# Splitting w_out into two float16 parts in place: the low part over the weights, the high part by a DMA, with the first stage in another order

## Chip, cores, metric

One core of a Trainium2 chip. The metric is the device time of one execution in microseconds. The core has TensorE (PE, matmuls, and its weight loads PEld), VectorE (DVE), ScalarE (ACT), GpSimd (POOL) and SyncE (SP), whose queue issues all DMAs of this kernel.

## What is computed

Attention in two steps, then a gated MLP with an RMS norm in front:

```python
q, k, v: (8 batches, 8 heads, 576 tokens, 64);  p: (8, 8, 32, 64)
packed = softmax(p @ k.T / 8) @ v               # 32 packed tokens a head
out    = softmax(q @ packed.T / 8) @ packed
x  = out.transpose(0, 2, 1, 3).reshape(4608, 512)
xn = x / sqrt(mean(x * x) + 1e-6) * rms_g
y  = (silu(xn @ w_gate) * (xn @ w_val)) @ w_out # 512 -> 1536 -> 512
```

The weights arrive as 64-bit floats and are read as pairs of 32-bit words; the result is float32.

## The kernel before

The 4608 tokens are worked through in 12 units of 384. For each unit there are a query load, an attention, and an MLP of 12 column blocks (`ft`) in six pairs (`c`). A batch has 576 tokens, so that some units need the packed tokens of two batches ("mixed" units). To keep float32 accuracy at float16 speed, each operand is split into a high and a low float16 part, and each product is made of three matmuls (high x high, high x low, low x high).

**The MLP.** The packed tokens are multiplied with the gate and value weights first (`packed_weights`, line 1217), and the result is split into `ring` (`pw_evict`, lines 455 and 457). The MLP's first part is the matmuls of line 1607; `gated` takes its results through silu (ACT, line 1658), a multiplication (DVE, line 1661), the high part (ACT, line 1681) and the low part (DVE line 1687 or POOL line 1684) into `hall`. The second part (line 1643) multiplies `hall` with `wo`, the two parts of w_out; `store` brings the result out (lines 1699 and 1702).

**Preparing the weights.** Each weight comes in pieces of 1 MB (twelve for gate and value, `gv_piece`, loads on line 530; six for w_out, `wo_piece`, loads on line 625). The raw words land in memory that is used later for something else (`ring`, `wo32` and `hall`; `RAW_AT` and `WO_AT` say which room). `to_f32` makes float32 of them: an ACT instruction (line 490), a POOL or DVE shift (lines 495 and 500; the lists `LOW` and `LOW_WO` choose) and a DVE merge (lines 497 or 502). Then come sums of squares for the scales. When all scales of w_out are known (`wo_scale`), `wo_split` makes the high and the low part of each of the six pieces: a scaling into a free `big` room (ACT line 690 or DVE line 693), the high part (ACT, line 699) and the low part (POOL, line 705). Both parts of a row lie in the 2,048 bytes that its float32 values had.

**Batches.** For each batch `keysets` loads p (line 734) and the keys in two halves (line 716) and turns them (early batches on PE, line 793, with evictions on line 800). `stage1` makes the packed tokens. The attention of a unit ends in `aTu` (line 1321), from which its MLP starts; lines 1513 to 1535 are its RMS norm on the way.

**The order.** Nothing is scheduled at run time: every engine's queue is written out in advance. Each piece of work is a generator (a chain) that yields what it wants next: an engine and an estimated time, a free buffer (a `Room` by name), or a mark set by another chain. `Plan.run` keeps an estimated clock for each engine and picks, among the chains that could start within a window (`CHOICE`) of the first, the one of the lowest rank (`RANK`, plus `LATER` times its number). The first dictionary of each pair is for the first stage (until unit 1's attention is planned), the second for the rest. `LATENCY`, `ACT_COST`, `DVE_COST`, `TABLE` and the like are its estimates; they change the order of instructions and nothing else. Where PE would idle in the first stage, `fill` puts in matmuls on constants (line 1731). `KEYS_AFTER` names the weight load after which batch 1's loads may be planned:

```python
if b == 1 and KEYS_AFTER:
    yield ("issued", KEYS_AFTER)
```

Loads 0 to 11 are the gate and value pieces, from 12 on those of w_out. There are six `big` rooms (p, keys, values, queries and their turned forms) and two `o` rooms (squares, and the stored results).

Of the kernel before, what the change touches and what calls it, by code (L numbers as in the profile page):

```python
# [9 lines left out]
F32 = mybir.dt.float32  # L10
F16 = mybir.dt.float16
# [3 lines left out]
AF = mybir.ActivationFunctionType  # L15
ALU = mybir.AluOpType
AX = mybir.AxisListType

P = 128
# [5 lines left out]
PE, ACT, DVE, POOL, LOAD, TPOSE = "pe", "act", "dve", "pool", "load", "tpose"  # L25

EXP, SILU = "exp", "silu"
# [3 lines left out]
    mybir.EngineType.SP,  # L31
)

LATENCY = {PE: 0.293, ACT: 0.16, EXP: 0.16, SILU: 0.16, DVE: 0.14, POOL: 0.022}
# [12 lines left out]

LOADING = (2.0, 320e3, 0.8)
TURNING = 2.2
# [3 lines left out]
def pe(n, count):  # L53

    return count * max(n / 2400 + 0.0025, 0.029)

ACT_COST = (0.076, 0.87e-3)
DVE_COST = (0.098, 0.953e-3)  # L60
# [173 lines left out]

RANK = ({"mlp": 1e9, "scales": 0.68, "gated": 0, "pw_evict": 0.42, "store": 0, "attention": 0.32, "stage1": 0.84, "keys": 0.49, "v": 0, "query": 0.55, "pw": 0.44, "g": 1.01, "w": 1.56, "wo": 0.96, "wo_split": 1.49, "conv": 2.38}, {"mlp": 1e9, "scales": 0.03, "gated": 0, "pw_evict": 0, "store": 0.25, "attention": 1.21, "stage1": 0.58, "keys": 0.27, "v": 0.78, "query": 0.42, "pw": 1.72, "g": 2.14, "w": 0.92, "wo": 2.54, "wo_split": 0.63, "conv": 2.76})
# [12 lines left out]
LOW_WO = "PPPDPP"  # L250

NORM_BY = "AAGAAAAAAAAA"
WO_SQ = "AAAAAA"
WO_BY = "ADADDD"
WO_LO = "PPPPPP"
KEYS_AFTER = 9
KEYS_BY = "ADAAAAADAADA"
QUERY_BY = "AADADA"
H_HI = "AAAAAAAAAAAA"
WO_HI = "AAAAAA"  # L260
H_LO = "DDDPPDDDDDDP"

H_LO_MIXED = "DDDDDDDDDDDD"
H_LO_ONE = "DDDDDDDDDDDD"


NORM_SLACK = (1.284, 3.0)

PW16_FROM = 8

# [16 lines left out]
def tile_packed_attention_then_swiglu(  # L287
# [36 lines left out]
    NFT = DF // P  # L324
# [101 lines left out]
    def tiny(n=1):  # L426

        r = plan.rooms["tiny"].pop(0)
        plan.rooms["tiny"].append(r)
        return r[1][:, :n, 0]  # L430

    def trio():
        r = plan.rooms["trio"].pop(0)
# [247 lines left out]
    def wo_split(i):  # L681
        yield "wo_sc",
        if H32:
            yield ("wo_free", i)
        st0 = yield Room("big")
        st = st0[:, : 2 * DM].rearrange("p (f n) -> p f n", f=2)
        hl = wo[:, 2 * i : 2 * i + 2]
        if WO_BY[i] == "A":
            yield ACT, act(1024)
            nc.scalar.activation(st, wo32[:, 2 * i : 2 * i + 2, :], AF.Copy, scale=wo_sc[:, i : i + 1])  # L690
        else:
            yield DVE, dve(1024) * 0.6
            nc.vector.tensor_scalar_mul(st, wo32[:, 2 * i : 2 * i + 2, :], wo_sc[:, i : i + 1])
        if WO_HI[i] == "D":
            yield DVE, 0.62
            nc.vector.tensor_copy(hl[:, :, 0, :], st)
        else:
            yield ACT, act(1024)
            nc.scalar.copy(hl[:, :, 0, :], st)
        if WO_LO[i] == "D":  # L700
            yield DVE, dve(1024)
            nc.vector.tensor_tensor(hl[:, :, 1, :], st, hl[:, :, 0, :], ALU.subtract)
        else:
            yield POOL, pool(1024)
            nc.gpsimd.tensor_tensor(hl[:, :, 1, :], st, hl[:, :, 0, :], ALU.subtract)
        plan.give("big", st0)
        plan.mark("wo_hl", i)


# [867 lines left out]
    def mlp():  # L1577
        for u in range(NU):
            yield ("aTu", u)
            if u == 0:  # L1580
                plan.warm = True
            sc, aT = units[u]
            for ft in range(NFT):
                c, f = divmod(ft, 2)
                for b, _, o, n in parts(u):
                    yield ("pw", b, c)
                yield ("sc", 0, c) if u == 0 else ("sc", u)
                pss, done = [], []
                for w in range(2):
                    ps = yield Room("pm")  # L1590
                    psi = ps[:, :UT].rearrange("p (i t) -> p i t", i=TPU)
                    yield PE, pe(UT, 8 if PW32 and u == 0 else 7 if PW32 and u == 1 else 6)
                    for b, _, o, n in parts(u):
                        pw = ring[:, slot_of(b, c)]
                        if PW32 and b == 0:
                            pw = pw.rearrange("p e l w f -> p e (l w f)").bitcast(F32)
                            x = aths[0] if u else whole(aT)
                            for g in range(2):
                                nc.tensor.matmul(
                                    psi[:, :, o : o + n], pw[:, g, 2 * P * w + f * P : 2 * P * w + (f + 1) * P], x[:, :, g, :],  # L1600
                                    start=(g == 0), stop=(g == 1),
                                )
                            continue
                        j = 0
                        for g in range(2):
                            for lw, la in ((0, 0), (0, 1), (1, 0)):
                                nc.tensor.matmul(  # L1607
                                    psi[:, :, o : o + n], pw[:, g, lw, w, f * P : (f + 1) * P], aT[:, :, la, g, o : o + n],
                                    start=(j == 0), stop=(j == 5),
                                )  # L1610
                                j += 1
                    pss.append(ps)
                    done.append(plan.now)
                plan.add(gated(u, ft, pss, done), "gated", u, ft)
                if f == 1:
                    for b, *_ in parts(u):
                        if (u + 1) * UT >= (b + 1) * S:
                            plan.mark("used", b, c)
            plan.give("aTu", aT)
            plan.mark("po", u)  # L1620
            for i in range(TPU):
                po = yield Room("pm")
                n = 0
                ts = slice(i * P, (i + 1) * P)
                if H32 and u == 0:
                    for ft in range(NFT):
                        if i == 0:
                            yield ("h", u, ft)
                            yield ("wo32", ft // 2)
                        yield PE, pe(DM, 4)  # L1630
                        nc.tensor.matmul(po, hall32[:, ft, ts], wo32[:, ft, :], start=(ft == 0), stop=(ft == NFT - 1))
                        if i == TPU - 1 and ft % 2:
                            plan.mark("wo_free", ft // 2)
                    plan.add(store(u, i, po), "store", u, i)
                    continue
                for ft in range(NFT):
                    if i == 0:
                        yield ("h", u, ft)
                        if u == (1 if H32 else 0):
                            yield ("wo_hl", ft // 2)  # L1640
                    yield PE, pe(DM, 3)
                    for lh, lw in ((0, 0), (0, 1), (1, 0)):
                        nc.tensor.matmul(po, hall[:, ft, lh, ts], wo[:, ft, lw, :], start=(n == 0), stop=(n == 3 * NFT - 1))  # L1643
                        n += 1
                plan.add(store(u, i, po), "store", u, i)

# [137 lines left out]
```

## Time and profile before

| | |
|---|---|
| median of 3 runs | 783.03 us (782.7 to 784.86) |
| the profiled execution | 781.74 us, its span 780.0 us |
| granted TensorE clock, mean | 0.987 |
| PE busy | 742.0 us (95%) |
| DVE busy | 497.2 us (64%) |
| ACT busy | 469.1 us (60%) |
| POOL busy | 55.5 us (7%) |

Times in the lines of the profile are microseconds from the span's start. In a timeline a row gives start, duration, engine, line, operation, what is written and read with the shapes, and in brackets how long the engine had idled and who released it. In the rows of waits stand who waited for whom, the sum, the number of times and the longest.

### The profile page before, as it was taken

Reading aid. Unit: us, or ns where it says so; the run is one execution under the profiler, and the core shown is the slowest. Engines: PE = TensorE matmul, PEld = TensorE weight load, DVE = VectorE, ACT = ScalarE, POOL = GpSimd, SP = SyncE. Lnnn points to the kernel's source line nnn. Section 1 sums busy time; section 2 is a strip of 40 time slices with the busy share of each in tenths; the row PEclk is TensorE's granted clock in tenths of the full one; section 3 lists DMA queues with packets and bytes.
Section 4 is the critical chain, followed back from the end, with each engine's and each line's share of the span. In section 5 each row is a group of like instructions: output and inputs, shape, how many; then the busy total and the mean of one; then the engine's idle time right before and its main releaser. Section 6 shows DMA issues by size and latency. Waiting matters only on the chain.

```text
span 780.0 us, 18192 instructions
## 1 busy us (share of the span) xinstructions
PE 742.0 (95%) x7653; PEld 433.5 (56%) x7653; DVE 497.2 (64%) x1086; ACT 469.1 (60%) x889; POOL 55.5 (7%) x55
## 2 busy tenths in 40 slices
PE   8756898999999999999999999999999999999998
PEld 6633463676445555477455555576554455685553
DVE  1798878586777486469467674688467365472341
ACT  3677877677778567288467756487366255371230
POOL 1433045000000000000000000000000000000000
PEclk9896999999999999999999999999999999999999
DMA  9998412545476437423832670837213213400001
GB/s 257 386 271 240 153 55 75 96 102 127 95 157 95 105 66 154 110 64 57 195 93 51 107 181 3 159 67 152 69 38 59 68 35 73 90 13 24 27 1 41
DMA packets 135506, 82.18 MB, mean 105 GB/s; under 512 B 98432, under 2 KB 123008, under 8 KB 135424
## 3 DMA queue, kind: packets, MB, share of 16 engines
q1 hardware_dynamic: 135424, 81.02, 44.2%
q8 instruction: 60, 0.98, 0.5%
q14 instruction: 22, 0.18, 0.1%
HBM read 47.97 MB, written 9.44 MB: 74 GB/s over the span
## 4 chain that ended last, share of the span: by engine, by line
PE 83%; DVE 6%; DMA 4%; SPq 3%; ACT 2%; issue 1%; DVEq 0%; ACTq 0%
PE pm_1x L1607 10%; PE pm_0x L1643 10%; PE pm_2x L1643 10%; PE pm_2x L1607 9%; PE pm_3x L1607 8%; PE pm_1x L1643 8%; PE pm_0x L1607 8%; PE pm_3x L1643 7%; SPq L530 2%; DMA hall<-in_moe_w_gate_dram 2%; PE pm_3x L1217 2%; PE pm_0x L1217 2%; PE quad L1426 1%; PE quad L1066 1%; PE pm_1x L1217 1%
## 5 line engine op out<-in xcount | busy, mean ns | idle before, releaser
L1607 PEld LDWEIGHTS <-ring 128*128 128x128 f16 x2304 | 204.7, 98 | 105.6 <-issue 33.6
L1643 PEld LDWEIGHTS <-hall 128*128 128x128 f16 x1296 | 124.1, 98 | 151.4 <-issue 11.7
L1643 PE MATMUL pm_0x<-wo,hall 128*128 128x512 f16 x360 | 82.2, 379 | 0.0
L1643 PE MATMUL pm_2x<-wo,hall 128*128 128x512 f16 x360 | 81.2, 379 | 0.0
L1643 PE MATMUL pm_3x<-wo,hall 128*128 128x512 f16 x288 | 65.2, 379 | 0.9 <-DVE t_1x L1661 0.9
L1643 PE MATMUL pm_1x<-wo,hall 128*128 128x512 f16 x288 | 65.1, 379 | 0.0
L1681 ACT CAST hall<-t_1x 128x384 f16<-128x384 f32 x72 | 36.7, 510 | 37.4 <-DVE t_1x L1661 36.9
L1607 PE MATMUL pm_1x<-aTu_0x,ring 128*128 128x192 f16 (+1 forms) x402 | 55.0, 281 | 1.2 <-DVE t_0x L1661 1.2
L1681 ACT CAST hall<-t_0x 128x384 f16<-128x384 f32 x72 | 36.5, 507 | 25.7 <-DVE t_0x L1661 25.4
L1687 DVE TENSOR_TENSOR hall<-t_1x,hall 128x384 f16<-128x384 f32 x70 | 38.9, 555 | 12.3 <-ACT hall L1681 10.4
L1687 DVE TENSOR_TENSOR hall<-t_0x,hall 128x384 f16<-128x384 f32 x71 | 39.7, 559 | 10.4 <-ACT hall L1681 10.2
L1607 PE MATMUL pm_2x<-aTu_0x,ring 128*128 128x384 f16 (+1 forms) x276 | 43.4, 298 | 0.0
L1607 PE MATMUL pm_0x<-aTu_1x,ring 128*128 128x384 f16 (+1 forms) x288 | 42.3, 289 | 1.0 <-DVE tiny_68x L963 1.0
L1607 PE MATMUL pm_2x<-aTu_1x,ring 128*128 128x192 f16 (+1 forms) x300 | 42.4, 285 | 0.6 <-DVE t_0x L1661 0.6
L1607 PE MATMUL pm_1x<-aTu_1x,ring 128*128 128x192 f16 (+1 forms) x300 | 42.3, 284 | 0.0
L1607 PE MATMUL pm_3x<-aTu_1x,ring 128*128 128x192 f16 (+1 forms) x264 | 37.8, 286 | 0.0
L1607 PE MATMUL pm_3x<-aTu_0x,ring 128*128 128x384 f16 (+1 forms) x240 | 35.5, 290 | 1.3 <-DVE t_0x L1661 0.9
L1607 PE MATMUL pm_0x<-aTu_0x,ring 128*128 128x192 f16 (+1 forms) x234 | 31.0, 277 | 1.6 <-ACT t_0x L1658 1.2
L1519 POOL TENSOR_TENSOR trio_2x<-trio_1x,neghalf 128x3 f32<-128x3 f32 x6 | 5.5, 916 | 280.9 <-DVE trio_1x L1513 280.9
L1519 POOL TENSOR_TENSOR trio_6x<-trio_5x,neghalf 128x3 f32<-128x3 f32 x6 | 5.1, 850 | 271.4 <-DVE trio_5x L1513 271.4
L1497 ACT ACTIVATE quad<-quad 128x512 f32<-128x512 f32 x36 | 21.1, 585 | 4.6 <-PE quad L1489 4.1
L457 DVE SCALAR_TENSOR_TENSOR ring<-pm_3x,pw_sc,ring 128x512 f16<-128x512 f32 x28 | 20.8, 744 | 3.8 <-ACT ring L455 3.8
(893 smaller groups left out, 1288.4 us busy)
## 6 DMA issues: line engine op xcount, KB each, us to landing
out_dram<-o_1x SPq DMA_DIRECT2D x18, 256.0 KB, 2.0
out_dram<-o_0x SPq DMA_DIRECT2D x18, 256.0 KB, 2.2
hall<-in_moe_w_out_dram SPq DMA_DIRECT2D x4, 1024.0 KB, 8.7
big_3x<-in_k_dram SPq DMA_DIRECT2D x7, 576.0 KB, 6.7
wo<-in_moe_w_gate_dram SPq DMA_DIRECT2D x3, 1024.0 KB, 15.5
wo<-in_moe_w_val_dram SPq DMA_DIRECT2D x3, 1024.0 KB, 13.0
big_2x<-in_k_dram SPq DMA_DIRECT2D x5, 576.0 KB, 6.3
big_1x<-in_v_dram SPq DMA_DIRECT2D x4, 576.0 KB, 7.3
```

The lines of the kernel that those rows point to most:

```text
L457: nc.vector.scalar_tensor_tensor(lo, x, s, hi, ALU.mult, ALU.subtract)
L530: nc.sync.dma_start(raw.rearrange("p k n e -> p k (n e)"), (w_gate, w_val)[n][:, 4 * c * P : 4 * (c + 1) * P].rearrange("(kt p) f -> p kt ...
L1066: nc.tensor.matmul(pp[32 * j : 32 * j + 32, :D], a1T[:, c, 32 * j : 32 * j + 32], vf[:, j, cv, :], start=(c == 0), stop=(c == NCK - 1),)
L1217: nc.tensor.matmul(ps[e][32 * j : 32 * j + 32, :], pg[h, j, :], wgv[h, c, j, :, :].rearrange("p w f -> p (w f)"), start=True, stop=True,)
L1426: nc.tensor.matmul(ps2[o : o + n, i, :, pi, :], qT[:, lq, i, pi, o : o + n], packs[b][3][:, lp, pi, :, :], start=(j == 0), stop=(j == 2),)
L1497: nc.scalar.activation(x, x, AF.Square, scale=2.0**-14, accum_out=ss[:, i : i + 1])
L1519: nc.gpsimd.tensor_tensor(ru, var, neghalf.broadcast_to([P, TPU]), ALU.pow)
L1607: nc.tensor.matmul(psi[:, :, o : o + n], pw[:, g, lw, w, f * P : (f + 1) * P], aT[:, :, la, g, o : o + n], start=(j == 0), stop=(j == 5),)
L1643: nc.tensor.matmul(po, hall[:, ft, lh, ts], wo[:, ft, lw, :], start=(n == 0), stop=(n == 3 * NFT - 1))
L1681: nc.scalar.copy(hall[:, ft, 0, :], t)
L1687: nc.vector.tensor_tensor(hall[:, ft, 1, :], t, hall[:, ft, 0, :], ALU.subtract)
```

## The change

`wo_split` no longer copies the scaled weights into a `big` room. ACT scales the piece and writes its high part into an `o` room; one DVE instruction multiplies the piece by its scale, subtracts the high part and writes the low part over the first half of each row of the weights; a DMA then brings the high part over the second half. The output matmuls read the two halves in the other order. Beside it, lists of which engine does what, the rooms of w_out's raw pieces, the place of batch 1's loads, the layout of the small scalars (`tiny`) and the planner's numbers are changed.

```diff
-CHOICE = ({'pe': 0.0, 'act': 0.458, 'dve': 0.275, 'pool': 0.476, 'sp': 1.005}, {'pe': 0.0, 'act': 0.417, 'dve': 0.087, 'pool': 0.208, 'sp': 0.274})
+CHOICE = ({'pe': 0.0, 'act': 0.458, 'dve': 0.275, 'pool': 0.298, 'sp': 0.833}, {'pe': 0.0, 'act': 0.382, 'dve': 0.13, 'pool': 0.269, 'sp': 0.274})
-AGE = (0.1, 0.078)
-TABLE = 1.735
+AGE = (0.1, 0)
+TABLE = 1.554
...
-RANK = ({"mlp": 1e9, "scales": 0.68, "gated": 0, "pw_evict": 0.42, "store": 0, "attention": 0.32, "stage1": 0.84, "keys": 0.49, "v": 0, "query": 0.55, "pw": 0.44, "g": 1.01, "w": 1.56, "wo": 0.96, "wo_split": 1.49, "conv": 2.38}, ...
-LATER = {"attention": -0.1, "stage1": -0.4, "keys": -0.05, "query": 0.0, "pw": -0.34, "w": 0.04, "wo": 0.0, "wo_split": 0.04}
+RANK = ({"mlp": 1e9, "scales": 0, "gated": 0, "pw_evict": 0.63, "store": 0, "attention": 0.16, "stage1": 0.84, "keys": 0.18, "v": 0, "query": 0.3, "pw": 0.44, "g": 1.01, "w": 1.45, "wo": 1.05, "wo_split": 1.49, "conv": 2.38}, ...
+LATER = {"attention": -0.78, "stage1": -0.4, "keys": 0.45, "query": 0.4, "pw": -0.46, "w": 0.34, "wo": 0.0, "wo_split": 0.02}
-WO_AT = (7, 8, 3, 8, 3, 8)
+WO_AT = (7, 3, 8, 7, 3, 8)
-VAL_BY = "DDPDDD"
+VAL_BY = "DDPADD"
-LOW_WO = "PPPDPP"
+LOW_WO = "PPPDDP"
-KEYS_AFTER = 9
+KEYS_AFTER = 12
-H_HI = "AAAAAAAAAAAA"
+H_HI = "AAAADAAAAADA"
-H_LO_MIXED = "DDDDDDDDDDDD"
+H_LO_MIXED = "DDDDPDDDDDDD"
...
-    rooms("tiny", 96, [P, 2, 2], F32)
+    rooms("tiny", 96, [P, 2], F32)
...
     def wo_split(i):
         yield "wo_sc",
-        st0 = yield Room("big")
-        st = st0[:, : 2 * DM].rearrange("p (f n) -> p f n", f=2)
-        hl = wo[:, 2 * i : 2 * i + 2]
...
-            nc.gpsimd.tensor_tensor(hl[:, :, 1, :], st, hl[:, :, 0, :], ALU.subtract)
-        plan.give("big", st0)
+        x, sc = wo32[:, 2 * i : 2 * i + 2, :], wo_sc[:, i : i + 1]
+        hi0 = yield Room("o")
+        hi = hi0.bitcast(F16).rearrange("p (f n) -> p f n", f=2)
+        yield ACT, act(1024)
+        nc.scalar.activation(hi, x, AF.Copy, scale=sc)
+        yield DVE, dve(1024)
+        nc.vector.scalar_tensor_tensor(wo[:, 2 * i : 2 * i + 2, 0, :], x, sc, hi, ALU.mult, ALU.subtract)
+        yield LOAD, P * 2048
+        nc.sync.dma_start(wo[:, 2 * i : 2 * i + 2, 1, :], hi)
+        plan.give("o", hi0)
...
-    nc.tensor.matmul(po, hall[:, ft, lh, ts], wo[:, ft, lw, :], ...)
+    nc.tensor.matmul(po, hall[:, ft, lh, ts], wo[:, ft, 1 - lw, :], ...)
```

More of the change, by code (lines that the diff above doesn't have):

```diff
@@ L32 @@
 )
-LATENCY = {PE: 0.293, ACT: 0.16, EXP: 0.16, SILU: 0.16, DVE: 0.14, POOL: 0.022}
+LATENCY = {PE: 0.299, ACT: 0.16, EXP: 0.16, SILU: 0.16, DVE: 0.14, POOL: 0.006}
 SLACK = (0.317, 0.223)
-CHOICE = ({'pe': 0.0, 'act': 0.458, 'dve': 0.275, 'pool': 0.476, 'sp': 1.005}, {'pe': 0.0, 'act': 0.417, 'dve': 0.087, 'pool': 0.208, 'sp': 0.274})
+CHOICE = ({'pe': 0.0, 'act': 0.458, 'dve': 0.275, 'pool': 0.298, 'sp': 0.833}, {'pe': 0.0, 'act': 0.382, 'dve': 0.13, 'pool': 0.269, 'sp': 0.274})
 IN_TURN = range(18)
 FILL = (0.9, 1.0, 400.0, 0.6)
-AGE = (0.1, 0.078)
-TABLE = 1.735
+AGE = (0.1, 0)
+TABLE = 1.554
 LOADING = (2.0, 320e3, 0.8)
@@ L55, in pe @@
     return count * max(n / 2400 + 0.0025, 0.029)
-ACT_COST = (0.076, 0.87e-3)
-DVE_COST = (0.098, 0.953e-3)
+ACT_COST = (0.081, 0.87e-3)
+DVE_COST = (0.068, 0.953e-3)
 def act(n):
@@ L233, in run @@
             self.go(chain)
-RANK = ({"mlp": 1e9, "scales": 0.68, "gated": 0, "pw_evict": 0.42, "store": 0, "attention": 0.32, "stage1": 0.84, "keys": 0.49, "v": 0, "query": 0.55, "pw": 0.44, "g": 1.01, "w": 1.56, "wo": 0.96, "wo_split": 1.49, "conv": 2.38}, {"mlp": 1e9, "scales": 0.03, "gated": 0, "pw_evict": 0, "store": 0.25, "attention": 1.21, "stage1": 0.58, "keys": 0.27, "v": 0.78, "query": 0.42, "pw": 1.72, "g": 2.14, "w": 0.92, "wo": 2.54, "wo_split": 0.63, "conv": 2.76})
-LATER = {"attention": -0.1, "stage1": -0.4, "keys": -0.05, "query": 0.0, "pw": -0.34, "w": 0.04, "wo": 0.0, "wo_split": 0.04}
+RANK = ({"mlp": 1e9, "scales": 0, "gated": 0, "pw_evict": 0.63, "store": 0, "attention": 0.16, "stage1": 0.84, "keys": 0.18, "v": 0, "query": 0.3, "pw": 0.44, "g": 1.01, "w": 1.45, "wo": 1.05, "wo_split": 1.49, "conv": 2.38}, {"mlp": 1e9, "scales": 0.03, "gated": 0, "pw_evict": 0, "store": 0.25, "attention": 1.21, "stage1": 0.58, "keys": 0.27, "v": 0.78, "query": 0.42, "pw": 1.83, "g": 2.14, "w": 0.92, "wo": 2.54, "wo_split": 0.63, "conv": 2.76})
+LATER = {"attention": -0.78, "stage1": -0.4, "keys": 0.45, "query": 0.4, "pw": -0.46, "w": 0.34, "wo": 0.0, "wo_split": 0.02}
 RAW_AT = (0, 1, 2, 3, 4, 5, 6, 7, 8, 4, 5, 6)
-WO_AT = (7, 8, 3, 8, 3, 8)
+WO_AT = (7, 3, 8, 7, 3, 8)
 EARLY_ROOMS = (5, 4, 3)
@@ L429, in tiny @@
         plan.rooms["tiny"].append(r)
-        return r[1][:, :n, 0]
+        return r[1][:, :n]
     def trio():
@@ L684, in wo_split @@
             yield ("wo_free", i)
-        st0 = yield Room("big")
-        st = st0[:, : 2 * DM].rearrange("p (f n) -> p f n", f=2)
-        hl = wo[:, 2 * i : 2 * i + 2]
[L688 to L705, printed above, removed]
-        plan.give("big", st0)
+        x, sc = wo32[:, 2 * i : 2 * i + 2, :], wo_sc[:, i : i + 1]
[8 more added lines that the diff above has]
+        plan.give("o", hi0)
         plan.mark("wo_hl", i)
@@ L1642, in mlp @@
                     for lh, lw in ((0, 0), (0, 1), (1, 0)):
-                        nc.tensor.matmul(po, hall[:, ft, lh, ts], wo[:, ft, lw, :], start=(n == 0), stop=(n == 3 * NFT - 1))
+                        nc.tensor.matmul(po, hall[:, ft, lh, ts], wo[:, ft, 1 - lw, :], start=(n == 0), stop=(n == 3 * NFT - 1))
                         n += 1
```

5 lines of the change are left out of this document (1 added, 4 removed).

## The prediction

> **What bounds the kernel now.** I read the page first, then the busy time of the engines by stage, then the waits, then the timelines of DVE, POOL, ACT and SP around the weight split. The span, and the stages (columns: busy us of PE, of its weight loads, of DVE, ACT and POOL, then granted clock, DMA share and GB/s):
>
> ```profile
> span 780.0 us, 18192 instructions
> ...
> 0.00:77.70 77.70, 56.07 (x654) 37.53 (x654) 53.81 (x129) 49.67 (x80) 26.24 (x33) 0.87 1.00 290
> 77.70:110.00 32.30, 28.58 (x342) 18.41 (x335) 25.29 (x57) 28.23 (x55) 5.30 (x5) 1.00 0.28 99
> 110.00:130.00 20.00, 15.75 (x94) 7.15 (x91) 16.73 (x22) 13.12 (x21) 13.76 (x7) 1.00 0.39 103
> 130.00:160.00 30.00, 29.66 (x373) 17.45 (x372) 21.48 (x50) 21.46 (x42) 1.28 (x2) 1.00 0.38 78
> 160.00:200.00 40.00, 36.71 (x530) 26.92 (x530) 29.14 (x70) 30.58 (x59) 0.85 (x1) 1.00 0.55 117
> 200.00:740.00 540.00, 538.93 (x5494) 307.89 (x5493) 339.69 (x743) 318.46 (x621) 8.01 (x9) 1.00 0.41 86
> 740.00:780.00 40.00, 36.30 (x188) 18.20 (x186) 11.11 (x19) 7.55 (x15) 0.00 (x0) 1.00 0.06 21
> ```
>
> The same for the filler matmuls alone (they only keep the array busy while nothing else is ready):
>
> ```profile
> 77.70:110.00 32.30, 3.27 (x27) 2.62 (x27) 1.00 0.28 99
> ```
>
> Subtract the PE column from each length: PE idles 21.63 us before 77.7, then 3.72, 4.25, 0.34, 3.29, 1.07 and 3.70. From 200 to 740 it has no room left, so a saved microsecond anywhere before is a microsecond of the total, and only the stretches before 200 and the tail can give one. The tail (last store) is not touched. What there is to win: 4.25 between 110 and 130, 3.29 between 160 and 200, 3.72 idle and 3.27 of filler between 77.7 and 110, and an earlier start of the first unit's MLP, which is this row of the PE timeline, the group of six matmuls beginning at 77.71:
>
> ```profile
> 77.71 1.20 PE L1607 MATMUL pm_3x<-aTu_0x,ring 128*128 128x384 f16 x6
> ```
>
> **The weight split itself (wo_split).** DVE around it, then POOL (columns: start, duration, engine, line, operation):
>
> ```profile
> 69.03 2.06 DVE L497 SCALAR_TENSOR_TENSOR wgv<-wgv,wo 128x1024 uint32<-128x1024 uint32 x1
> ...
> 100.34 1.22 DVE L497 SCALAR_TENSOR_TENSOR wo<-wo,hall 128x1024 uint32<-128x1024 uint32 x1 [0.28 <-POOL hall L495]
> ...
> 107.93 0.74 DVE L693 TENSOR_SCALAR big_0x<-wo,wo_sc 128x1024 f32<-128x1024 f32 x1
> ...
> 110.72 1.55 DVE L693 TENSOR_SCALAR big_4x<-wo,wo_sc 128x1024 f32<-128x1024 f32 x1
> 112.19 2.61 DVE L693 TENSOR_SCALAR big_5x<-wo,wo_sc 128x1024 f32<-128x1024 f32 x1
> ...
> 117.70 2.49 DVE L693 TENSOR_SCALAR big_2x<-wo,wo_sc 128x1024 f32<-128x1024 f32 x1
> ...
> 121.16 3.29 DVE L1153 SCALAR_TENSOR_TENSOR pbd<-pts_0x,tiny_47x,pbd 64x128 f16<-64x128 f32 x2
> ```
>
> ```profile
> 68.88 1.14 POOL L495 TENSOR_SCALAR hall<-hall 128x1024 uint32<-128x1024 uint8 x1 [3.52 <-DMA hall<-in_moe_w_out_dram]
> ...
> 111.68 2.58 POOL L705 TENSOR_TENSOR wo<-big_0x,wo 128x1024 f16<-128x1024 f32 x1
> 117.37 2.27 POOL L705 TENSOR_TENSOR wo<-big_3x,wo 128x1024 f16<-128x1024 f32 x1 [3.11 <-DMA pf_0x<-in_p_dram]
> 119.60 2.57 POOL L705 TENSOR_TENSOR wo<-big_4x,wo 128x1024 f16<-128x1024 f32 x1
> 122.13 2.17 POOL L705 TENSOR_TENSOR wo<-big_5x,wo 128x1024 f16<-128x1024 f32 x1
> ...
> 128.30 2.13 POOL L705 TENSOR_TENSOR wo<-big_2x,wo 128x1024 f16<-128x1024 f32 x1
> ```
>
> The same L693 takes 0.74 us while POOL is quiet and 1.55, 2.61 and 2.49 us beside a POOL subtraction; the 2.61 one ends at 114.80, 0.54 after POOL's 114.26. The two small L1153 take 3.29 together and end at 124.45, when POOL's fifth subtraction ends (124.30). So POOL's subtractions cost DVE 0.81 + 1.87 + 1.75 = 4.43 us on L693 and most of 3.29 on L1153. PE waits there for what queues behind them on DVE:
>
> ```profile
> PE pm_1x L1607 <- DVE t_0x L1661: 1.2, 1, 1.2
> PE pm_3x L1643 <- DVE t_1x L1661: 0.9, 1, 0.9
> ```
>
> The change takes all six POOL subtractions away. DVE's four L693 (0.74 + 1.55 + 2.61 + 2.49 = 7.39 us) become six multiply-subtracts of 1024 elements. Their nearest row is L497: 1.22 us quiet, 2.06 beside POOL's L495 at 68.88. I take 1.22, as POOL has little left at that place: 7.3 us, so DVE's own sum is even and L1153 is freed of its 2 to 3 us. Of the 4.25 us that PE idles here I count 3.0 as won, at most 4.25, at least nothing (the other waits, for ACT's silu, stay).
>
> The Trainium skill, "SBUF — State Buffer", section "Who interferes with whom", says that a DVE instruction with two SBUF inputs is blocked by a GpSimd instruction that reads SBUF, for the whole instruction. That speaks against the new multiply-subtract: its weights and its high part both lie in SBUF, so by it each could be held behind the POOL instructions that remain. The 2.06 row agrees; if the rule caught all six, the sum would rise by 6 x 0.84 = 5.0 us of DVE, and as few POOL instructions remain here I leave it out of the sum.
>
> ACT: two scalings and six casts become six casts with a scale. Their nearest row:
>
> ```profile
> 108.47 1.04 ACT L699 CAST wo<-big_1x 128x1024 f16<-128x1024 f32 x1
> ```
>
> By it ACT saves two instructions, some 2 us, hidden (ACT is idle 6.9 us between 110 and 130): 0.
>
> The high part goes by six DMAs of 256 KB between SBUF addresses. Nearest is the store of the same size:
>
> ```profile
> out_dram<-o_1x SPq DMA_DIRECT2D x18, 256.0 KB, 2.0
> ```
>
> A piece then passes ACT 1.04, DVE 1.22, DMA 2.0, about 4.3 us; two rooms "o" let two pieces run at once, so six need 3 x 4.3 = 13 us against 22.5 before (107.93 to 130.43). PE's output matmuls are the cover: they can begin on the first pieces. Should a DMA take double, the split needs 19 us, still within 22.5. But each copy heads SP's queue until its DVE instruction is done, and what is queued behind waits along: loads for unit 2 and batch 2, the first unit's stores. I take +0.5, between 0 and +3 (half a copy's wait, 2.3 us, and the store's issue).
>
> The Trainium skill, "DMA: Bandwidth & Descriptors", section "Bandwidth", measures 138 GB/s for 64 KB and 341 GB/s for 1 MB; between them I estimate some 250 GB/s, 1.05 us for 256 KB, beside its fixed cost of about 2 us ("Latency and other measured facts"). That is 3 us a copy where the row says 2.0, and the split 16 us instead of 13, with the sum unchanged; no run so far shows an SBUF-to-SBUF copy.
>
> **What the rooms release.** Before, the split took all six "big" rooms; SP stood still for them:
>
> ```profile
> SPq L1343 <- POOL wo L705: 17.6, 1, 17.6
> ...
> SPq L716 <- POOL wo L705: 7.5, 2, 5.4
> ```
>
> ```profile
> 122.20 0.31 SPq L716 DMA_DIRECT2D big_4x<-in_k_dram  x1
> ```
>
> That last row is batch 2's second half of keys, and batch 2's softmax is what PE waits for later:
>
> ```profile
> 174.48 1.15 PE L1607 MATMUL pm_0x<-aTu_1x,ring 128*128 128x192 f16 x12 [1.00 <-DVE tiny_68x L963]
> ...
> 189.74 0.39 PE L1527 MATMUL quad<-ru_0x,ones 128*128 128x3 f32 x2 [1.06 <-DVE tiny_69x L948]
> ```
>
> With the rooms free earlier these two waits (2.06 of the 3.29 us) can go. I count 1.5 won; bounds 3.3 won and 3 lost (see the rival with the keys).
>
> **First stage anew.** KEYS_AFTER goes from 9 to 12, so batch 1's four p loads and two key loads move past the last two gate/value pieces and the first piece of w_out:
>
> ```profile
> 44.12 0.31 SPq L716 DMA_DIRECT2D big_3x<-in_k_dram  x1
> ...
> 51.60 3.02 SPq L625 DMA_DIRECT2D hall<-in_moe_w_out_dram  x2
> ```
>
> ```profile
> 44.12 8.71 DMA big_3x<-in_k_dram
> ```
>
> The keys then start at about 54 instead of 44, 10 us later, and land at about 63 instead of 52.83; the weight pieces behind come some 3 us sooner (two halves of 576 KB, 1.18 MB, at the first stage's mean of 290 GB/s would be 4). The attention of unit 0 ranks higher, and that is where the start of the MLP is decided:
>
> ```profile
> 59.06 0.21 DVE L1513 TENSOR_SCALAR trio_1x<-trio_0x,eps 128x3 f32<-128x3 f32 x1
> ...
> 72.33 0.94 DVE L1321 SCALAR_TENSOR_TENSOR aTu_0x<-quad,aTu_0x 128x768 f16<-128x768 f32 x1
> ```
>
> Between these two lie 13.3 us for a handful of short steps, because DVE is busy with other pieces (53.81 of 77.7). I take the MLP's start 2 us earlier and 1.5 us of it kept; bounds 6 won (half of the 13.3) and 3 lost (the reordering delays a piece that the first group needs).
>
> **Small edits.** One more w_out piece is shifted by DVE instead of POOL, two high parts of hall go from ACT to DVE, one scaling of w_val from DVE to ACT:
>
> ```profile
> 91.68 0.68 DVE L500 TENSOR_SCALAR wo<-wo 128x1024 uint32<-128x1024 uint32 x1
> ```
>
> On DVE that is +0.68 for the shift, two casts of 384 elements of at most 0.74 each (L693's for 1024), and -0.74: at most +1.4, in a stretch where DVE idles 32.30 - 25.29 = 7.0 us. I take +0.5; without that cover it is 1.4. One multiply in twelve of the mixed units goes to POOL, the tiny tile is packed, and stage two gets other choices: 0, since PE is full there, with +-1 for the 1.07 us that it idles.
>
> **Sum:** -3.0 - 1.5 - 1.5 + 0.5 + 0.5 = -5.0 us. The profiled execution took 781.74 us, 1.29 under the median of 783.03; 781.74 - 5.0 = 776.7, and with the 1.29 a median of **778.0**. About 0.3%, 2.4 us, is what a measurement of this kernel can tell from no change.
>
> **Rivals.** *The keys come too late (slower).* Batch 1's keys land 10 us later. The cover is that batch 1's work has some 97 us between its keys' landing and unit 1's MLP, most of it waiting for its turn on DVE and ACT behind unit 0. But the last step left little:
>
> ```profile
> 149.69 0.94 DVE L1321 SCALAR_TENSOR_TENSOR aTu_1x<-quad,aTu_1x 128x768 f16<-128x768 f32 x1
> ```
>
> ```profile
> 152.78 1.15 PE L1607 MATMUL pm_0x<-aTu_1x,ring 128*128 128x192 f16 x12
> ```
>
> Unit 1's operand was ready at 150.63, 2.2 us before its MLP began; batch 2 follows batch 1 and had no slack. It decides from a delay of about 5 us on: if 8 of the 10 us reach unit 1 and batch 2, PE idles 8 - 2.2 = 5.8 more, against some 1.7 won elsewhere: 783 + 4 = 787.
>
> *The gap only moves (same).* The DVE time taken out equals that put in, and between 110 and 130 PE also waits for ACT; if the freed DVE time only brings PE to the next wait (the exp/silu table switch, the hi copies), less than half of the sum stays: 782.
>
> *The first MLP starts much earlier (much faster).* If the new order brings the 13.3 us between the two rows above down by 6 and the rest of the sum holds, 778 - 4.5 = 773.5, and with all of the 4.25 and 3.29 gone 771.
>
> *By the port rule* above, remaining POOL work holding all six: 783.
>
> **Chances.** The forecast (775 to 780.6) 0.42, much faster 0.23, only moved or held by the port 0.20, keys late 0.15. So faster 0.65, same 0.20, slower 0.15. The likeliest one's own range is 775 to 781. The range to give: below, all of the 4.25 and 3.29 and 6 for the start, 783.0 - 13.5 = 769.5; above, the keys' rival, 786.5.
>
> **What would show it.** Right: no POOL subtraction after 105; every 1024-element multiply-subtract near 1.22; PE idle between 110 and 130 near 1 us; the loads for unit 2 and batch 2 before 111; MLP start near 75.5. Wrong: MLP start later than 78; PE waiting for batch 1 or 2 between 130 and 200 by more than 3.3 us; high-part copies landing after 130; SP's queue standing on them while a load behind it is needed.

## The result, and the profile after

The changed kernel takes 790.88 us (median of 4 runs, 788.86 to 791.47) against 783.81 us for the kernel before (four runs; the first three gave the 783.03 above): ratio 1.010, interval 1.008 to 1.012. Forecast was 778.0 us, so it went the other way: 7 us slower instead of 5 faster. The profiled span is 788.4 us, 8.4 above the 780.0 of before. The same stages of the changed kernel (columns as in the prediction's first fence):

```profile
span 788.4 us, 18226 instructions
...
0.00:77.70 77.70, 57.30 (x660) 37.01 (x661) 54.49 (x131) 51.97 (x83) 27.89 (x33) 0.91 1.01 296
77.70:110.00 32.30, 29.10 (x300) 18.20 (x301) 27.52 (x59) 30.78 (x54) 2.96 (x3) 1.00 0.26 101
110.00:130.00 20.00, 17.93 (x283) 10.24 (x282) 17.77 (x38) 13.86 (x26) 1.34 (x1) 1.00 0.57 156
130.00:160.00 30.00, 27.98 (x278) 15.02 (x278) 17.51 (x39) 17.08 (x34) 0.86 (x1) 0.89 0.40 87
160.00:200.00 40.00, 39.27 (x435) 28.01 (x435) 26.91 (x58) 27.09 (x54) 2.27 (x2) 1.00 0.44 97
200.00:740.00 540.00, 532.13 (x5478) 304.14 (x5477) 335.10 (x738) 312.97 (x614) 11.50 (x12) 1.00 0.41 87
```

Length minus the PE column: PE idles 20.40, 3.20, 2.07, 2.02, 0.73 and 7.87 us, before it was 21.63, 3.72, 4.25, 0.34, 3.29 and 1.07. The front gained everywhere except between 130 and 160, where there is new idle time and a granted clock of 0.89; and from 200 on, where before PE had no room left, 7.87 us are idle. The stores say the same. SP's timeline, last store of unit 1, of unit 9, and of the whole; first before, then after:

```profile
220.60 0.83 SPq L1702 DMA_DIRECT2D out_dram<-o_0x  x1
...
678.05 0.33 SPq L1702 DMA_DIRECT2D out_dram<-o_0x  x1
...
777.11 0.33 SPq L1702 DMA_DIRECT2D out_dram<-o_0x  x1
```

```profile
216.57 0.36 SPq L1688 DMA_DIRECT2D out_dram<-o_1x  x1
...
686.43 0.33 SPq L1688 DMA_DIRECT2D out_dram<-o_1x  x1
...
785.38 0.33 SPq L1688 DMA_DIRECT2D out_dram<-o_1x  x1
```

At unit 1's end the changed kernel is 4.03 us ahead; at unit 9's it is 8.38 behind and stays so. (A store's time also depends on what the order puts ahead of it, so a single offset isn't a price.) From unit 1's last store to unit 9's, the stage that the prediction put at 0, the changed kernel falls back by 12.4 us.

PE's longest wait in the changed kernel, from the view of waits (in order of their sums), is one that isn't in the kernel before. "issue" says that PE waited for nothing that the profile shows:

```profile
PE quad L1475 <- issue: 3.8, 1, 3.8
...
PE pm_3x L1593 <- issue: 1.5, 1, 1.5
```

The place of the first in the timelines of weight loads and of PE:

```profile
126.89 1.26 PEld L1475 LDWEIGHTS <-aT_0x 32*64 32x64 f16 x144 [0.42 <-ACT ring L452]
```

```profile
128.05 0.21 PE L1475 MATMUL quad<-pav_1x,aT_0x 32*64 32x64 f16 x1
132.02 0.21 PE L1475 MATMUL quad<-pav_3x,aT_0x 32*64 32x64 f16 x1 [3.77 <-issue]
```

Line 1475 is the attention of a mixed unit: 144 weight loads and 144 matmuls of 32x64, 288 instructions in 1.26 us. PE stops one matmul short of the burst's end and resumes 3.77 us later, though the last matmul needs no more than the one before it. What moved meanwhile is a transfer of queue q8, which brings instructions. The page of the profile counts its packets; below it the same queue between 128.9 and 129.6 with the line of GB/s in 40 slices of 17.5 ns (a packet's bytes all stand in the slice in which it begins):

```profile
q8 instruction: 60, 0.98, 0.5%
```

```profile
GB/s 351 263 88 176 351 263 176 264 263 88 263 176 351 88 88 264 88 176 88 88 176 88 176 0 176 88 0 0 0 0 0 936 0 0 0 0 0 0 0 0
...
q1 hardware_dynamic: 69, 0.08, 51.8%
q8 instruction: 1, 0.02, 10.1%
```

60 packets carry 0.98 MB, 16 KB each. Of the 18,226 instructions PE has 15,328 matmuls and weight loads and 40 others, about 256 for each packet: the burst eats more than a packet's worth in 1.26 us. The packet begins at 129.45 amid data of another queue; 10.1% of 16 engines over 0.7 us are 1.13 us, so it ends at 130.57, and PE resumes 1.4 us later. Another stop follows the same kind of burst at 635.6. Between 635.8 and 636.6 only the instruction packet moves (from 636.45, for 0.92 us), and PE resumes 1.4 us after its end:

```profile
GB/s 0 0 0 0 0 0 0 0 0 0 0 0 0 0 0 0 0 0 0 0 0 0 0 0 0 0 0 0 0 0 0 0 819 0 0 0 0 0 0 0
...
q8 instruction: 1, 0.02, 7.2%
```

```profile
638.77 1.45 PE L1593 MATMUL pm_3x<-aTu_1x,ring 128*128 128x384 f16 x5 [1.49 <-issue]
```

Counting shows where PE stops. In the changed kernel 2,497 PE instructions have begun before the first stop, 9,921 before a short one of 0.69 us at 489.84, and 13,250 before the one of 1.49 us. The later two lie 29 and 42 times 256 behind the first, to one instruction, and 29 and 42 packets came in between. The same holds for every wait of a PE matmul on "issue" of over 0.3 us in all runs of this case, ten in seven kernels: each stands a whole multiple of 256 instructions from 2,497, to one instruction, and as many packets on. So PE stops at the end of a block of 256 instructions and resumes when the packet with the next block has landed. The kernel before has its 2,497th instruction in the same burst and doesn't stop there: the packet began at 135.29, 1.4 us ahead of the burst (136.71), whereas in the changed kernel it begins 2.6 us behind the burst's start.

Two of the stops cost more than themselves, as PE comes back at a lower clock (two stretches after the first stop, and one after the stop of 1.49 us):

```profile
132.00:136.00 4.00, 3.98 (x22) 0.79 (x22) 2.20 (x8) 3.07 (x8) 0.58 (x1) 0.50 0.18 68
136.00:140.00 4.00, 4.00 (x19) 1.76 (x17) 1.32 (x7) 1.35 (x4) 0.28 (x1) 0.83 0.69 132
...
640.00:644.00 4.00, 4.00 (x18) 2.09 (x17) 1.68 (x3) 1.69 (x4) 0.00 (x0) 0.68 0.01 4
```

With clocks of 0.50 and 0.83, PE did 4 x 0.50 + 4 x 0.17 = 2.7 us less work than at full clock. The Trainium skill, "TensorE: Matmul & The Clock Gate", Part 1, gives half rate after about 3.4 us without work; the 0.50 behind 3.77 us agrees, but behind the stop of 1.49 us the granted clock fell to 0.50 as well, from 639.2 to 642.5 (the 0.68 is the mean over 4 us), and there the measurement decides. Behind the stop of 0.69 us it stayed at 1.00.

### The profile page after: what moved, and what is told of

Read it like the earlier page. It is cut to its first block, busy times and chain, and to the rows that moved or that the text cites. A ratio compares the mean times of both kernels' runs of the same rounds, so it can differ in the third digit from the quotient of the medians.

```text
span 788.4 us, 18226 instructions
## 1 busy us (share of the span) xinstructions
PE 748.3 (95%) x7664; PEld 435.8 (55%) x7664; DVE 495.6 (63%) x1086; ACT 465.3 (59%) x884; POOL 46.8 (6%) x52
## 4 chain that ended last, share of the span: by engine, by line
PE 72%; DVE 7%; ACT 5%; issue 3%; DMA 2%; SPq 0%; DVEq 0%; ACTq 0%
PE pm_2x L1629 9%; PE pm_1x L1629 9%; PE pm_0x L1629 9%; PE pm_0x L1593 8%; PE pm_2x L1593 7%; PE pm_1x L1593 7%; PE pm_3x L1629 6%; PE pm_3x L1593 6%; PE pm_3x L1203 1%; PE quad L1412 1%; PE quad L1052 1%; DVE ring L454 1%; PE pm_2x L1203 1%; PE quad L1475 1%; DVE t_0x L1647 1%
## 5 line engine op out<-in xcount | busy, mean ns | idle before, releaser
L1629 PE MATMUL pm_1x<-wo,hall 128*128 128x512 f16 x396 | 90.2, 382 | 0.0
L1629 PE MATMUL pm_0x<-wo,hall 128*128 128x512 f16 x324 | 73.4, 379 | 0.0
L1629 PE MATMUL pm_3x<-wo,hall 128*128 128x512 f16 x252 | 57.2, 382 | 0.0
L1593 PE MATMUL pm_0x<-aTu_0x,ring 128*128 128x192 f16 (+1 forms) x360 | 50.4, 283 | 1.5 <-ACT t_1x L1644 1.0
L1593 PE MATMUL pm_0x<-aTu_1x,ring 128*128 128x192 f16 (+1 forms) x300 | 42.7, 286 | 0.4 <-DVE t_0x L1647 0.2
L1593 PE MATMUL pm_1x<-aTu_0x,ring 128*128 128x384 f16 (+1 forms) x264 | 40.1, 293 | 0.5 <-DVE ring L454 0.2
L1593 PE MATMUL pm_2x<-aTu_0x,ring 128*128 128x192 f16 (+1 forms) x288 | 40.1, 283 | 0.0
L1593 PE MATMUL pm_3x<-aTu_1x,ring 128*128 128x384 f16 (+1 forms) x252 | 38.4, 294 | 1.5 <-issue 1.5
L452 ACT ACTIVATE ring<-pm_3x,pw_sc 128x512 f16<-128x512 f32 x31 | 21.1, 681 | 4.6 <-PE pm_1x L1203 4.0
L454 DVE SCALAR_TENSOR_TENSOR ring<-pm_1x,pw_sc,ring 128x512 f16<-128x512 f32 x24 | 17.9, 747 | 7.4 <-ACT ring L452 7.0
```

The costliest lines, as they stand in the source:

```text
L452: nc.scalar.activation(hi, x, AF.Copy, scale=s)
L454: nc.vector.scalar_tensor_tensor(lo, x, s, hi, ALU.mult, ALU.subtract)
L1593: nc.tensor.matmul(psi[:, :, o : o + n], pw[:, g, lw, w, f * P : (f + 1) * P], aT[:, :, la, g, o : o + n], start=(j == 0), stop=(j == 5),)
L1629: nc.tensor.matmul(po, hall[:, ft, lh, ts], wo[:, ft, 1 - lw, :], start=(n == 0), stop=(n == 3 * NFT - 1))
```

## The experiments

The theories when the runs began: (A) the second stage's new numbers (`RANK`, `CHOICE`, `AGE`, estimates) cost the time; (B) the in-place split costs it, through the copies on SP; (C) PE's instruction stream runs dry behind the bursts of tiny matmuls, worse when the loads of batch 2's keys hold up the fetch. All ratios are to the kernel before, run beside it on the same chip (medians 782.6 to 783.3 us).

**Which part of the change.** The changed kernel with the old second stage, and the other way round:

```
e1: after; RANK[1], CHOICE[1], AGE[1], H_LO_MIXED and the estimates
    LATENCY/TABLE/ACT_COST/DVE_COST in the second stage as before
e2: before; the same numbers, new ones in the second stage
```

> The changed kernel, but the planner's numbers for everything planned after unit 1's attention (second entries of RANK, CHOICE and AGE, the cost and latency estimates from there on, and H_LO_MIXED) are those of before; the first stage is the changed one. Theory A (the loss lies in the order of the second stage, whose units 2 to 9 took 12.3 us more than before after a lead of 4.0 us at the end of unit 1): 777 to 783. Theory B (the split in place with its DMA costs it): stays at 789 to 792. Theory C (the first stage's 3.8 us stall of PE at 128 us and the cold clock behind it): stays at 789 to 792, with the stall still in the trace.

> The kernel before with only the changed numbers for what is planned after unit 1's attention; first stage and split as before. Theory A: 791 to 796 (the 8 to 12 us appear here). Theories B and C: 783 to 785, as before.

e1: 782.51 us, 1.0002 [0.9991, 1.0013]. e2: 837.08 us, 1.068 [1.067, 1.070], with PE waiting up to 10.98 us for one DMA of `aTu`. So the numbers of the second stage matter, but not as a cost that one could add: they belong to the order that stands before them. And e1 still has the first stop, now 3.52 us, but none behind it.

**The split.** In place in the kernel before, and the old split in the changed kernel, both with the order planned anew:

```
e3: before + new wo_split, lw -> 1 - lw
e4: after + old wo_split, 1 - lw -> lw
```

> The kernel before with only the split of w_out in place (ACT high part into an o room, DVE low part over the weights, DMA of the high part, the output matmuls' halves swapped); all numbers of the planner and all lists as before. My prediction's terms for the split (3.0 for the port, 1.5 for the rooms, minus 0.5) say 778 to 781. Theory B: 786 to 792. Theory A: at or below the kernel before, 778 to 784.

> The changed kernel with the old split (big room, POOL subtraction, no DMA); all else as changed. Theory A: still slow, 790 to 797, since what the split won is lost on top. Theory B: back to 781 to 785.

e3: 796.51 us, 1.017 [1.015, 1.018]; e4: 789.54 us, 1.008 [1.007, 1.010]. Every edit of a step gives a new order of everything, so neither isolates the split. Neither has a stop of the kind above (the longest wait on "issue" is 0.2 us), so an order can also be slow without one. To measure it alone, e7 keeps every queue's order of the kernel before and puts the new instructions in the places of the old:

```
-  POOL: tensor_tensor(wo low, big, wo high, subtract)
+  DVE:  scalar_tensor_tensor(wo low, x, sc, big)     # same place
+  SP:   dma_start(wo high, big)                      # same place
```

> The kernel before with the split of w_out in place, but with the order frozen: the planner is asked for the same engines, times and rooms as before, so that every queue keeps its order; the scaling is left out, ACT writes the high part with its scale, DVE's multiply-subtract and the DMA stand where POOL's subtraction was planned, and the high part lies in a big room. My prediction's term for POOL's port alone: 3.0 won, 779 to 782. Theory B (the split in place costs, by its DMAs or by DVE): 785 to 792. If the 13.9 us of POOL work were hidden, and DVE's time even: 782 to 784.

e7: 787.28 us, 1.006 [1.004, 1.008]. The stretch 110 to 125 of before, then of e7:

```profile
110.00:125.00 15.00, 11.04 (x66) 5.68 (x63) 14.60 (x18) 9.41 (x16) 11.19 (x5) 1.00 0.47 125
```

```profile
110.00:125.00 15.00, 14.37 (x118) 7.32 (x115) 13.75 (x25) 10.84 (x18) 0.00 (x0) 1.00 0.36 110
```

PE idles 0.63 us instead of 3.96: without POOL's subtractions DVE gives back 3.3 us, the prediction's first term (3.0). PE runs the same instructions in the same order in both; laid side by side, e7 goes from 0.9 us behind at 110 to 3.3 ahead at 127, so that the gain is 4.2. By the Trainium skill, "SBUF — State Buffer", "Who interferes with whom", a DVE instruction with two SBUF inputs contends with a GpSimd instruction that reads SBUF; the trace doesn't contradict it, as the six multiply-subtracts take 1.27 or 1.28 us with POOL at 0.00. But then PE stands for a copy; PE's and SP's timelines of e7:

```profile
134.83 2.72 PE L1632 MATMUL pm_3x<-wo,hall 128*128 128x512 f16 x6 [5.71 <-DMA wo<-big_2x]
```

```profile
121.31 0.55 SPq L1332 DMA_DIRECT2D big_1x<-in_q_dram  x1
...
126.84 0.37 SPq L705 DMA_DIRECT2D big_3x<-in_k_dram  x1
127.33 0.40 SPq L705 DMA_DIRECT2D big_4x<-in_k_dram  x1
127.85 0.60 SPq L694 DMA_DIRECT2D wo<-big_2x  x1
```

The last copy goes out at 127.85, behind the loads that the copies ahead held back (the query load went out at 111.75 before, now at 121.31), and PE starts on it 7.0 us later; another wait takes 1.6 us. Two ways around it:

```
e12: e7; unit 2's query load and batch 2's key loads behind the last copy
e13: e7; nc.gpsimd.dma_start for the copies
```

> The frozen-order split in place, in which PE waited 5.7 us for the last copy of the high part (issued at 127.85 behind 1.9 MB of loads for unit 2 and batch 2, landed at 134.8): the query load of unit 2 and the key loads of batch 2 now stand behind the last copy in SP's queue, everything else as there. If the copies' place in SP's queue was the loss: the waits fall to 1 us or less and the port's gain shows, 778.5 to 781.5. If the DMA itself is the loss, wherever it stands: 785 to 788.

> The frozen-order split in place, but the six copies of the high part are issued from POOL's queue, where the subtraction stood, instead of SP's. If the loss of 4.7 us was loads and copies waiting for one another in SP's queue: unit 2's query load goes out at about 112 again, no wait of PE for a copy over 1 us, and the port's gain shows: 778.5 to 781. If the copies' transfers collide with the loads on the DMA engines whoever issues them: 784 to 788.

e12: 785.22 us, 1.003 [1.002, 1.005]; e13: 784.77 us, 1.002 [1.000, 1.003]. In e12 PE waits only 0.40 and 1.41 us for copies, and 3.37 us for what the late query load feeds: the loss moves from the copies to the loads. In e13 the loads no longer wait for copies at SP, but PE still waits 1.91 and 3.64 us for copies:

```profile
126.62 0.72 POOL L694 DMA_DIRECT2D wo<-big_5x  x1 [2.59 <-issue]
```

```profile
133.26 2.75 PE L1632 MATMUL pm_3x<-wo,hall 128*128 128x512 f16 x12 [3.64 <-DMA wo<-big_5x]
```

6.6 us from issue to landing, on another queue: the copies meet the 1.2 MB of keys on the DMA engines, not only in SP's queue. Side by side with the kernel before, e7 falls back by 4.7 us between 110 and 140, e12 by 2.1 and e13 by 0.1: in the old order the copies give back all that the split won. (What e13 is slower by in its profile, 3.2 us, it has lost before 110, ahead of any copy.) In the changed kernel's own order the copies go ahead of these loads and PE waits for none of them.

**The stop.** Two ways to move it from the burst, both on e1 so that the second stage is that of before:

```
e5: batch 2's two key loads issued behind unit 0's first store (SP only)
e6: filler() emits nothing in its first 40 calls (80 PE instructions fewer)
```

> The kernel of the run with the second stage's old numbers, in which PE stands still for 3.5 us at 128 us behind the 144 tiny matmuls of unit 1's attention, with nothing that the profile shows as its reason. Only batch 2's two key loads are moved in SP's queue, behind the first store (from about 123 to about 134 us); every engine's order is otherwise the same. Theory P (PE's next block of instructions is fetched by the same DMA engines, and its fetch at 129 us stood behind those 1.2 MB): the stall shrinks to 1.5 us or less, and the time falls by 2 to 5, to 777.5 to 780.5. Theory Q (the tiny burst outruns the fetch whatever the DMAs do): stall and time stay, 781.5 to 784. If the later keys cost batch 2 something, PE waits longer in unit 2: up to 788.

> The same kernel as the run with the second stage's old numbers, but without the first 40 filler matmuls (80 instructions of PE, all before 8 us, where PE waits for its first data): every later instruction of PE lies 80 places further ahead in the blocks in which its instructions are fetched; the order is the same. Theory Q: the burst at 127 us no longer meets two ends of a block, the stall goes, 776 to 779 (another burst may meet them instead: then it shows there and the time stays). Theory P: the stall stays near 3.5 us, 781.5 to 784.

e5: 778.66 us, 0.996 [0.994, 0.998]. e6: 777.99 us, 0.995 [0.993, 0.997], the lowest median of all. PE at the burst's end in e1, e5 and e6:

```profile
131.85 0.21 PE L1481 MATMUL quad<-pav_3x,aT_0x 32*64 32x64 f16 x1 [3.52 <-issue]
```

```profile
128.45 0.18 PE L1486 MATMUL quad<-pav_3x,aT_0x 32*64 32x64 f16 x1 [1.07 <-issue]
```

```profile
129.10 0.21 PE L1481 MATMUL quad<-pav_3x,aT_0x 32*64 32x64 f16 x1
```

e1 and e5 write out the same stream of PE instructions. In e1 the instruction packet begins 2.4 us after the burst's start (129.36 against 126.96), amid key loads (128.9 to 129.6 in 40 slices; the packet is the slice with 1024):

```profile
GB/s 263 439 88 263 263 263 527 0 176 263 351 263 264 88 176 263 264 88 351 88 264 176 263 88 88 176 1024 0 351 0 88 0 176 0 0 88 0 0 176 0
...
q1 hardware_dynamic: 90, 0.12, 75.8%
```

In e5 it begins 0.2 us after the burst's start (126.24 against 126.02) and takes 0.96, with the DMA engines otherwise idle (125.6 to 126.4 in 40 slices):

```profile
GB/s 0 0 0 0 0 0 0 0 0 0 0 0 0 0 0 0 0 0 0 0 0 0 0 0 0 0 0 0 0 0 0 0 819 0 0 0 0 0 0 0
...
q8 instruction: 1, 0.02, 7.5%
```

So 3.52 - 1.07 = 2.45 us of the stop is the fetch standing behind the keys, and 1.07 us the burst itself: both theories hold in part. In e6 the packet begins at 130.4, after the burst (127.93 to 129.19), which runs through without it: with 80 instructions fewer ahead, the block that ended at the burst's end now ends at 134.8. (e6 has one short stop left, 0.52 us at 634.1, again at a block's end.) That the loss is one of position and not of work is also shown by the same shift on the changed kernel (40 fillers, and 20) and on the kernel before:

```
e9: after, first 40 fillers not emitted     e10: the first 20
e11: before, first 40 fillers not emitted
```

> The changed kernel itself, without the first 40 filler matmuls: order as changed, PE's instructions lie 80 places further ahead. If its loss is PE running out of fetched instructions behind tiny bursts (3.8 us at 128 us, 0.7 at 490, 1.5 at 637, each with a slow clock behind it): the stall at 128 goes, 783 to 787 if the others stay, 779 to 782 if they go too. If the order of the second stage is slow in itself: 789 to 792.

> The same with 20 filler matmuls left out, 40 places. If stalls come and go with where the bursts lie in the fetched blocks: another time within 779 to 792, and its trace shows a PE pause without a shown reason behind a tiny burst for every stretch that is long. If the shift as such gained (less PE work at the start): the same as with 40, within 1 us.

> Control: the kernel before without the first 40 filler matmuls. Its trace shows no such pause, so the shift can gain nothing: 782 to 784; slower, up to 790, if a burst now meets the ends of two blocks.

e9: 781.66 us, 0.9986 [0.997, 1.000]. e10: 783.05 us, 1.000 [0.999, 1.002]. All three stops are gone in both, and with them 9.2 and 7.8 us of 790.88. The stretch of the first stop, in the changed kernel and in e9:

```profile
128.00:132.00 4.00, 0.26 (x31) 0.15 (x19) 1.05 (x2) 0.00 (x0) 0.00 (x0) 0.82 0.35 80
```

```profile
128.00:132.00 4.00, 4.00 (x158) 1.99 (x137) 3.62 (x11) 3.22 (x9) 0.33 (x1) 1.00 0.65 172
```

Behind the fillers PE's instructions are the same in both, so they can be laid side by side. e9 gains 6.4 us on the changed kernel at the first stop and its slow clock, 0.9 at the second and 3.3 at the third, and loses 1.3 us in all the rest: the whole difference lies at the stops. In e9 a block ends near the start of the first burst instead of at its end, and its packet had begun 11 us ahead. e11: 784.43 us, 1.002 [1.000, 1.004]: leaving fillers out is no gain in itself, and there it brings a stop of 0.73 us at 642.6 that the kernel before hasn't.

**The second stage.** What is left between e9 and e6, 3.7 us by the medians and 3.1 by the ratios, are the second stage's numbers. Taken apart:

```
e8:  after; only RANK[1], CHOICE[1], AGE[1] old
e14: e9; only H_LO_MIXED old
e15: e9; only the estimates of the second stage old
```

> The changed kernel with only RANK, CHOICE and AGE of the second stage as before; its cost and latency estimates and the POOL entry in H_LO_MIXED stay as changed. If the ranks and windows carry the loss of units 2 to 9: 781 to 784, like the run with all of the second stage's numbers old. If the estimates of cost or the POOL entry do: 788 to 792.

> The changed kernel without 40 fillers (781.7) with only H_LO_MIXED back to all DVE. If the one low part on POOL in mixed units carries the 3.7 us: 777.5 to 779.5. If the estimates or ranks do: 781 to 783. A new pause without a shown reason behind a tiny burst would add 3 to 6 and be seen in the trace.

> The changed kernel without 40 fillers (781.7) with only the estimates of cost and latency of the second stage as before. If they carry the 3.7 us: 777.5 to 779.5. If the POOL entry or the ranks do: 781 to 783. A new pause behind a tiny burst would add 3 to 6.

e8: 792.61 us, 1.014 [1.012, 1.017]; its first stop is 3.82 us and there is a new one in a later unit's burst, of 4.13 us, again with key loads on the DMA engines, and with the clock at 0.50 behind it:

```profile
468.86 0.26 PE L1481 MATMUL quad<-pav_3x,aT_0x 32*64 32x64 f16 x1 [4.13 <-issue]
```

```profile
468.00:472.00 4.00, 3.14 (x58) 1.70 (x59) 0.00 (x0) 1.03 (x3) 0.00 (x0) 0.50 0.02 4
```

e14: 781.12 us, 0.997 [0.996, 0.998], as e9: the low part that POOL got (a subtraction; the prediction calls it a multiply) costs nothing that can be seen. e15: 808.04 us, 1.031 [1.028, 1.034], with this wait among others:

```profile
519.36 2.08 PE L1600 MATMUL pm_2x<-aTu_1x,ring 128*128 128x192 f16 x12 [11.12 <-DMA aTu_1x<-hl_0x]
```

Single groups of the numbers thus can't be priced; only the whole set can, at 3 to 4 us. One wait that e9 has there, and the changed kernel in the same way:

```profile
432.94 0.88 PE L1052 MATMUL quad<-big_5x,a1T_0x 96*32 96x64 f32 x48 [1.75 <-ACT a1T_0x L1040]
```

Which of the numbers makes the rest stays open.

**Copies from POOL in the best order.** e6 with `nc.gpsimd.dma_start` for the six copies:

> The fastest so far (first stage as changed, second stage's numbers old, 40 fillers less: 778.0) with the six copies issued from POOL's queue. If copies in SP's queue still hold loads back there: 776 to 777.5. If the new order had already room for them: 777.5 to 778.5. Slower, 779 to 781, if issuing on POOL takes longer and PE's output matmuls wait for a copy.

779.08 us, 0.995 [0.992, 0.997]: not to be told from e6. Where copies aren't behind loads, no difference shows between the two queues; they land in 2.5 us (median) here too.

## Why the prediction was wrong, point by point

- **A term that the sum lacked.** This is the step that failed. No step asked whether PE gets its instructions in time, so the sum put that wait at nothing. Among PE's waits of before none is for "issue"; the same burst, there at 136.71, goes through whole (row below), as the packet it needs had begun 1.4 us ahead of it. In the changed order the fetch starts in the burst, with key loads on its path. Stops of 3.77, 0.69 and 1.49 us and the slow clock behind two of them make the 7.8 to 9.2 us that e9 and e10 win back: more than the whole slowdown. This is shown by e5 (the load moved, PE's stream kept), by e6, e9 and e10 (the stream moved) against e11, and by the place of every stop at a block's end.

```profile
136.71 1.26 PEld L1489 LDWEIGHTS <-aT_0x 32*64 32x64 f16 x144 [0.42 <-ACT big_0x L455]
```

- **"Stage two gets other choices: 0, since PE is full there, with +-1."** Mis-sized: +3.7 us by the medians (e9 781.66 against e6 777.99), beside the two stops in that stage. A PE that is full shows that there is nothing to win; it says nothing on what another order can lose. The bound upwards was wrong.
- **POOL's subtractions, -3.0 us.** Right in its mechanism, and measured at 3.3 to 4.2 in e7. In the changed kernel the multiply-subtracts take 1.28 where 1.22 was put, and the two small instructions that took 3.29 take 0.70:

```profile
109.52 1.28 DVE L689 SCALAR_TENSOR_TENSOR wo<-wo,wo_sc,o_1x 128x1024 f16<-128x1024 f32 x1
...
122.94 0.70 DVE L1139 SCALAR_TENSOR_TENSOR pbd<-pts_0x,tiny_47x,pbd 64x128 f16<-64x128 f32 x2
```

  PE's 2.07 us of idle time between 110 and 130 are the stop but for 0.3; "near 1 us" was too cautious. The port rule's rival did not come either: two multiply-subtracts overlap a POOL instruction (at 119.22 in the changed kernel, at 124.50 in e7) and still take 1.28 and 1.27 us, while POOL's subtraction takes 1.34 both times, where it took 0.92 at 96.15 in the changed kernel.
- **The copies on SP, +0.5 us.** Within its bounds for the order that the planner made: PE waits for none, and e16 finds no difference. Wrong as a price of the copy itself: in the order of before they cost 1.6 and 5.7 us (e7), outside the bound of +3, because a copy of 2.0 us by the store's row took up to 6.9 us behind loads.
- **The rooms, -1.5 us.** The idle time between 160 and 200 fell by 2.56 us, but not for the reason given. Unit 2's query load goes out at 111.52, as before (111.75), and batch 2's keys later than before, not ahead of 111. The rooms no longer hold them back, but in SP's queue they stand behind copies, as the prediction had feared for its +0.5:

```profile
110.83 0.59 SPq L691 DMA_DIRECT2D wo<-o_1x  x1
111.52 0.56 SPq L1329 DMA_DIRECT2D big_1x<-in_q_dram  x1
...
120.56 0.59 SPq L691 DMA_DIRECT2D wo<-o_1x  x1
...
123.32 0.38 SPq L702 DMA_DIRECT2D big_3x<-in_k_dram  x1
123.79 0.42 SPq L702 DMA_DIRECT2D big_4x<-in_k_dram  x1
```

  What freed the stretch from 160 to 200 instead wasn't tested.
- **The MLP's start, -1.5 us.** The size was low: it starts at 73.03, 4.7 us earlier where 2 were taken. That is more than chance: it starts between 72.4 and 75.4 in every profile with the new first stage, and between 77.7 and 80.6 in every one with the old. The rival of late keys did not come: but for the stop, no wait in PE's timeline between 130 and 200 is longer than 0.21 us.

```profile
73.03 2.08 PE L1593 MATMUL pm_3x<-aTu_0x,ring 128*128 128x384 f16 x6 [0.28 <-DVE ring L454]
```

- **The sum.** With the stop moved away and the second stage as before (e6) the kernel takes 777.99 us, some 5 us less than before, as the prediction's sum has it. That the sum comes out is partly luck: the start and POOL's subtractions gave more than was counted, and from 200 to 740 PE still idles 4.21 us in e6, where it was 1.07 and "+-1" was allowed. e5 and e6, the new first stage and split with the old second stage and the stop moved, beat both kernels: the one before by 0.4 and 0.5%.

## What to carry to other kernels

Where hundreds of tiny matmuls follow each other in a microsecond, PE's instructions are a stream with a bandwidth of its own: look in the waits for "issue" behind such a burst, count whether a block of 256 PE instructions ends in the burst or just behind it, and see which transfers share the DMA engines with the fetch just then. A few instructions more or less ahead of the burst, or a load issued 7 us later, can be worth more than the edit that one is pricing; so test a changed order with a shift before blaming the edit. And price a re-planned order with a bound for loss that is as wide as the whole stage is sensitive, not by the idle time that is left in it.

## What the runs showed of the hardware

- PE's instructions come in 16 KB packets of 256 over the DMA engines that also carry the data. All ten stops of over 0.3 us stand at a block's end. PE resumed 1.2 to 1.6 us after the packet's end (e5 127.20 to 128.45, the changed kernel 130.57 to 132.02). A burst of 288 instructions in 1.26 us can outrun this: behind such bursts the stops were 0.5 to 1.5 us with the DMA engines free of loads in the last microsecond before the packet, and 3.5 to 4.1 us with key loads on them. Which instruction makes a fetch due isn't in the trace.
- A stop of 1.49 us behind such a burst was enough to lower the granted clock to 0.50 for 3.4 us; behind stops of 0.69 and 1.07 us (e5) it stayed at 1.00.
- A 256 KB copy within SBUF landed in 2.5 us in the changed kernel, and in 6.6 (POOL's queue, e13) to 6.9 us (SP's, e7) amid 1.2 MB of key loads:

```profile
wo<-o_1x SPq DMA_DIRECT2D x1, 256.0 KB, 2.5
```
